# Down's first load as 116 rows and three times four rows, instead of 128 rows at once

## The chip, the cores and the metric

The kernel runs on one core of one Trainium2 chip. The metric is the device time of one execution in microseconds (us). A core has a matrix engine (PE), a vector engine (DVE), a scalar engine (ACT), GpSimd (POOL) and a queue engine (SP); loads from device memory are issued by SP or ACT and carried out by sixteen DMA engines that belong to the core.

## The reference

One token goes through a transformer block: a modulated layer norm, attention over a cache of 16384 keys and values for 32 heads, a second modulated layer norm, and a gated feed-forward part. Only the last line matters for the change.

```python
mod = (_silu(c) @ w_mod).reshape(c.shape[0], 6, 1, -1)
sa, ca, ga, sb, cb, gb = (mod[:, 0].copy(), ..., mod[:, 5].copy())
h = _layernorm(x, axis=-1) * (1 + ca) + sa
x = x + ga * _A_ref(h, A_k_cache, A_v_cache, A_wq, A_wo)      # attention; x is 1 x 1 x 640
h = _layernorm(x, axis=-1) * (1 + cb) + sb
g = _silu(h @ w_gate); u = h @ w_up                           # 640 x 1728 each
x = x + gb * (g * u @ w_down)                                 # w_down: 1728 x 640, "Down"
```

All matrices and the caches are bf16. The two caches are 134 MB each; the matrices together are about 22 MB.

## The kernel before, in words

The heads are worked in 16 pairs. A pair's keys (`kring`, two buffers) and values (`vbuf`) arrive as tiles of 128 partitions with 64 KB on each. DVE multiplies the keys by the query and folds the products, PE finishes the sums, ACT takes the exponentials, and PE weighs the values. PE's work on the pairs is a loop, and DVE's and ACT's from the third pair on.

All weights and caches are loaded by `dma` (line 83), which issues one load on SP's queue and gives it a semaphore of its own; the line that the profile names for every load is 90. SP issues in the order of the program and waits, ahead of a load, until its destination is free. The program has 44 such loads, all of 128 partition rows: w_mod, Wq, the first keys in two pieces, 15 more of keys, 16 of values, Wo in two pieces (line 631), Gate (642), Up (644) and five of Down (646 to 652). ACT issues the loads of `c` and `x`, one row each, and the second of the two stores of the result, which have two rows each (lines 770 and 771).

The tail is what the change touches. When the last keys have been reduced (`o_R[15]`), their buffer is free, and SP issues Gate, Up and the five loads of Down one behind the other (`wdeps`, line 641). Down's 1728 rows are cut by `BLOCKS` and `DOWN`. Each of the first three loads brings 512 rows of `w_down`, four to a partition: 128 partition rows of four times 640 values of two bytes, 5120 bytes each, 640 KB in all. The fourth has one row of `w_down` on each partition (160 KB), and the fifth has the last 64 rows, cut in half (80 KB).

Meanwhile PE weighs the last values, projects by Wo (line 679), and does Gate and Up (line 716). DVE makes `gu_col` from them (line 746). Then line 758 multiplies by Down in five parts, `down0` to `down4`; part i waits for load i. The first three parts have 16 matmuls each, the fourth and fifth have 4. `twice_gu` (763) and `gu_half` (765), which only `down4` needs, follow `down0`. DVE multiplies by the gate and adds the residual (767, 768), and SP and ACT each store half of the 640 results.

Of the kernel before, what the change touches and what calls it, by code (L numbers as in the profile page):

```python
# [37 lines left out]
class _Plan:  # L38
# [38 lines left out]
    def op(self, eng, fn, deps=(), name="", chan=None):  # L77
        o = _Op(eng, fn, list(deps), name, len(self.ops), self.loop.get(eng), chan)
        o.sig = chan is not None
        self.ops.append(o)  # L80
        return o

    def dma(self, out_ap, in_ap, key, deps=(), name="", eng="sp", noncontig=False):
        nc = self.nc

        def fn(e, out_ap=out_ap, in_ap=in_ap, noncontig=noncontig):
            if noncontig:
                with nc.allow_non_contiguous_dma(reason="tiny vector layout change"):
                    return e.dma_start(out_ap, in_ap)
            return e.dma_start(out_ap, in_ap)  # L90

        return self.op(eng, fn, deps, name, chan=self.dma_chan(key))
# [116 lines left out]
def build(nc, A_x, A_k, A_v, A_wq, A_wo, B_wg, B_wu, B_wd, c_in, w_mod, out):  # L209
# [13 lines left out]
    BLOCKS = [(0, 4, 0), (512, 4, 4), (1024, 4, 8), (1536, 1, 12)]  # L223

    DOWN = [(0, 0, 4), (1, 0, 4), (2, 0, 4), (3, 0, 1), (None, 0, 0)]
    FCH = NF + 1
    QW = 32
    QR = 16
# [4 lines left out]
    with es:  # L233
        plan = _Plan(nc, es)
        op, dma = plan.op, plan.dma
        POOL, ACT, DVE, PE = "pool", "act", "dve", "pe"

        def sb(name, shape, dtype):
            return es.enter_context(nc.sbuf_tensor(name, list(shape), dtype))
# [56 lines left out]
        ab = sb("ab", [128, KC, 2], BF16)  # L296
        g_sb = sb("g_sb", [128, FCH], F32)
        eg = sb("eg", [128, FCH], F32)
        dg = sb("dg", [128, FCH], F32)
        rg = sb("rg", [128, FCH], F32)  # L300
        sg = sb("sg", [128, FCH], F32)
        gu_col = sb("gu_col", [128, FCH], BF16)
        gu_half = sb("gu_half", [128, 2], BF16)
# [116 lines left out]
        def wide(col):  # L420
            return col.broadcast_to([col.shape[0], 32])
# [11 lines left out]
        def pick(half, n, o_m, free):  # L433
# [14 lines left out]
            deps=[o_m0, o_xn], name="t1")  # L448
# [11 lines left out]
        for g in range(H // 4):  # L460
            b = g % 2
# [9 lines left out]
            for half in range(2):  # L471
# [4 lines left out]
                    deps=[o_q[g]], name="qbc%d_%d" % (g, half)))  # L476
# [5 lines left out]
        o_R, o_pv, o_exp, o_nb, o_mx, o_acc, o_ot = ([None] * NP for _ in range(7))  # L482
# [141 lines left out]
        PL = NP - 1  # L624
# [16 lines left out]
        wdeps = [o_R[NP - 1]]  # L641
# [3 lines left out]
        d_wd = []  # L645
        for i, (b, r0, r1) in enumerate(DOWN):
            if b is None:
                dst, src = wt_v, B_wd[NF * 128:F, :].rearrange("q (h n) -> (q h) n", h=2)
            else:
                f0, n, j0 = BLOCKS[b]  # L650
                dst, src = wd_v[:, j0 + r0:j0 + r1, :], B_wd[f0:f0 + 128 * n, :].rearrange("(p r) n -> p r n", r=n)[:, r0:r1, :]
            d_wd.append(dma(dst, src, ("wd", i), deps=wdeps, name="dma_wd%d" % i))

# [2 lines left out]
                 deps=[o_exp[PL], o_rz, o_onesf, o_rstd], name="L")  # L658
# [7 lines left out]
                  deps=[o_z, o_e32] + o_qev[-2], name="am")  # L666
# [21 lines left out]
        def f_cols(e):  # L688
# [14 lines left out]
            deps=[o_ga, o_xf], name="x1")  # L703
# [18 lines left out]
        def gate0(o_xc1):  # L722
# [6 lines left out]
            deps=[o_xc1, o_rstd1, o_onep_b], name="t2")  # L729
# [6 lines left out]
                  deps=[o_xsp, o_ot[PL], o_strips], name="x1_rows")  # L736
# [9 lines left out]
        o_gum = op(DVE, lambda e: e.tensor_tensor(out=gu_col[:], in0=u_ps[:, 0:FCH], in1=sg[:], op=ALU.mult), deps=[o_sg, o_u], name="gu")  # L746
        for i, (b, r0, r1) in enumerate(DOWN):

            if b is None:
                work = [(gu_half[:, r // 2:r // 2 + 1], wt_v[:, RW * (r % 2):RW * (r % 2) + RW], r) for r in range(4)]  # L750
            else:
                j0 = BLOCKS[b][2]
                work = [(gu_col[:, j:j + 1], wd_v[:, j, RW * r:RW * r + RW], r) for j in range(j0 + r0, j0 + r1) for r in range(4)]

            def f_down(e, i=i, work=work):
                last = None
                for at, (col, rows, r) in enumerate(work):
                    last = e.matmul(f_ps[32 * r:32 * r + 32, 0:RW], lhsT=wide(col), rhs=rows, start=(i == 0 and at < 4),  # L758
                                    stop=(i == len(DOWN) - 1 and at >= len(work) - 4), tile_position=(0, 32 * r))
                return last  # L760
            prev = op(PE, f_down, deps=[o_gum if b is not None else o_guh, d_wd[i], o_nb[PL]], name="down%d" % i)
            if i == 0:
                o_tw = op(PE, lambda e: e.matmul(attn_ps[:, 8:9], lhsT=twice[64:128].rearrange("p q h -> p (q h)"), rhs=gu_col[64:128, NF:FCH], start=True, stop=True),
                          deps=[o_gum, o_twice, o_abf], name="twice_gu")
                o_guh = op(DVE, lambda e: e.tensor_tensor(out=gu_half[:], in0=attn_ps[:, 8:9].broadcast_to([128, 2]), in1=even[:], op=ALU.mult),
                           deps=[o_tw, o_even], name="gu_half")
# [10 lines left out]
def bass_adaLN_cond__gqa_block_cached__swiglu_ffn__decode_kernel(  # L777
    nc: bass.Bass,
    A_x: bass.AP,
    A_k_cache: bass.AP,  # L780
    A_v_cache: bass.AP,
    A_wq: bass.AP,
    A_wo: bass.AP,
    B_x: bass.AP,
    B_w_gate: bass.AP,
    B_w_up: bass.AP,
    B_w_down: bass.AP,
    c: bass.AP,
    w_mod: bass.AP,
    out: bass.AP,  # L790
):
    build(nc, A_x, A_k_cache, A_v_cache, A_wq, A_wo, B_w_gate, B_w_up, B_w_down, c, w_mod, out)
# [28 lines left out]
```

## Time and profile before

| | before |
|---|---|
| median of 3 runs | 679.24 us (678.79 to 679.37) |
| the profiled execution | 678.87 us |
| its span, first to last instruction | 677.6 us |
| DVE busy | 514.1 us (76%) |
| PE busy | 363.6 us (54%) |
| DMA: bytes, mean rate | 290.58 MB, 429 GB/s |
| DMA packets | 6355 |

The page of the profile gives busy time by engine, the span in 40 slices, the DMA queues with their packets, and the chain of work that ended last. Busy shares are of the span. A packet is one piece that one DMA engine moves; the end mark that tells a semaphore that the engine is done is a packet of 4 bytes. The DMA share of a window is the mean over the sixteen engines, so that 1.00 means that all are busy and 0.25 that four are, or that all are busy a quarter of the time. Windows and the timeline count from the span's start.

### The profile page before, as it was taken

What the parts mean: (1) busy time and instruction counts of PE and PEld (TensorE: products, weight loads), DVE (VectorE), ACT (ScalarE), POOL (GpSimd) and SP (SyncE); (2) the same over time, 40 slices, a digit from 0 to 9 for tenths busy, and PEclk for the clock granted to TensorE, in tenths of its full rate; (3) what the DMA queues carried; (4) which work ended last, traced back from release to release, by engine and by line L of the source; (5) the groups of instructions that cost most, each with busy time, mean ns of one, the idle gap of its engine ahead of it and who ended that gap; (6) DMA issues with size and microseconds to landing.
All of it is one profiled execution on the core that took longest, in us unless ns stands there. A gap on an engine that the chain in (4) does not pass through costs nothing.

```text
span 677.6 us, 5406 instructions
## 1 busy us (share of the span) xinstructions
PE 363.6 (54%) x2069; PEld 144.5 (21%) x2069; DVE 514.1 (76%) x190; ACT 46.4 (7%) x146; POOL 0.7 (0%) x6
## 2 busy tenths in 40 slices
PE   2420475755728284654818375562828465481776
PEld 1100122221212122221302122121212222130335
DVE  2189997959596896959597795959699695959912
ACT  1120000100000000000000010000000000000010
POOL 0000000000000000000000000000000000000000
PEclk9675565555757565565756556575656556565765
DMA  9999999999999999999999999999999999999997
GB/s 375 440 459 433 433 437 430 433 430 433 433 434 433 433 433 433 433 433 433 433 433 433 433 433 433 433 433 433 433 433 433 433 433 433 433 433 433 430 400 318
DMA packets 6355, 290.58 MB, mean 429 GB/s; under 512 B 714, under 2 KB 972, under 8 KB 1356
## 3 DMA queue, kind: packets, MB, share of 16 engines
q1 hardware_dynamic: 6340, 290.48, 99.3%
q8 instruction: 5, 0.08, 0.0%
q14 instruction: 2, 0.02, 0.0%
q10 hardware_dynamic: 8, 0.00, 0.0%
HBM read 290.47 MB, written 0.00 MB: 429 GB/s over the span
## 4 chain that ended last, share of the span: by engine, by line
DMA 49%; DVE 30%; issue 13%; PE 8%; SPq 0%; DVEq 0%
DMA kring<-in_A_k_cache_dram 45%; DVE kring L544 10%; PE psb L534 7%; DVE kring L549 6%; DVE kring L562 5%; DVE kring L568 5%; DMA kring<-in_B_w_down_dram 4%; DVE kring L554 3%; SPq L90 0%; DVE pm L581 0%; DVE nb L589 0%; PE psb L576 0%; PE psb L758 0%; DVEq L191 0%; DVEq L544 0%
## 5 line engine op out<-in xcount | busy, mean ns | idle before, releaser
L544 DVE TENSOR_TENSOR kring<-kring,qbc 128x16384 bf16<-128x16384 bf16 x28 | 243.3, 8690 | 96.1 <-DMA kring<-in_A_k_cache_dram 96.1
L534 PE MATMUL psb<-kring,ident 128*128 x448 | 197.5, 607 | 120.3 <-DVE kring L554 120.3
L549 DVE TENSOR_TENSOR kring<-kring 128x8192 bf16<-128x8192 bf16 x28 | 123.8, 4421 | 0.5
L534 PEld LDWEIGHTS psb<-kring,ident 128*128 128x128 bf16 x448 | 54.0, 120 | 248.0 <-issue 247.2
L508 PE MATMUL psb<-vbuf,PZ 128*8 128x512 bf16 x960 | 80.9, 511 | 0.0
L585 PE MATMUL psb<-d,bd_f 128*128 128x64 f32 x32 | 11.0, 446 | 118.5 <-ACT d L583 118.5
L554 DVE TENSOR_TENSOR kring<-kring 128x4096 bf16<-128x4096 bf16 x28 | 64.1, 2288 | 0.5
L562 DVE TENSOR_TENSOR kring<-kring,qbc 128x16384 bf16<-128x16384 bf16 (+2 forms) x5 | 34.9, 6981 | 23.4 <-DMA kring<-in_A_k_cache_dram 23.4
L508 PEld LDWEIGHTS psb<-vbuf,PZ 128*8 128x8 bf16 x960 | 26.6, 108 | 58.9 <-issue 49.0
L576 PE MATMUL psb<-kring,ident 128*128 128x256 bf16 (+3 forms) x64 | 14.5, 392 | 43.2 <-DVE kring L568 43.2
L585 PEld LDWEIGHTS psb<-d,bd_f 128*128 128x128 f32 x32 | 8.0, 312 | 120.7 <-DVE pm L581 111.3
L568 DVE TENSOR_TENSOR kring<-kring 128x2048 bf16<-128x2048 bf16 (+7 forms) x15 | 32.2, 2148 | 0.4
L523 PEld LDWEIGHTS psb<-sel,acc_sb 128*128 128x128 f32 x128 | 28.5, 311 | 7.7 <-issue 4.3
L523 PE MATMUL psb<-sel,acc_sb 128*128 128x2 f32 x128 | 25.6, 322 | 1.1 <-ACT acc_sb L514 1.1
L514 ACT ACTIVATE acc_sb<-psb 128x512 f32<-128x512 f32 x16 | 9.6, 598 | 210.7 <-PE psb L508 210.7
L593 ACT ACTIVATE PZ<-psb,nb 64x256 bf16<-64x256 f32 x32 | 15.0, 469 | 64.8 <-DVE nb L589 64.6
L576 PEld LDWEIGHTS psb<-kring,ident 128*128 128x128 bf16 x64 | 6.4, 121 | 50.5 <-DVE kring L568 44.3
L583 ACT ACTIVATE d<-negid,pm 128x64 f32<-128x64 f32 x16 | 5.6, 348 | 153.2 <-DVE pm L581 153.2
L466 PE MATMUL psb<-vbuf,h_col 128*128 128x512 bf16 x40 | 10.9, 443 | 8.6 <-DMA vbuf<-in_A_wq_dram 8.6
L527 ACT ACTIVATE OT_sb<-psb 128x2 f32 (+1 forms) x16 | 2.8, 172 | 152.2 <-PE psb L523 152.2
L581 DVE TENSOR_REDUCE pm<-psb 128x1 f32<-128x256 f32 x16 | 6.7, 419 | 1.2 <-PE psb L576 1.2
L466 PEld LDWEIGHTS psb<-vbuf,h_col 128*128 128x128 bf16 x40 | 4.1, 112 | 15.3 <-DMA vbuf<-in_A_wq_dram 9.0
(105 smaller groups left out, 79.2 us busy)
## 6 DMA issues: line engine op xcount, KB each, us to landing
kring<-in_A_k_cache_dram SPq DMA_DIRECT2D x2, 4096.0 KB, 40.1
vbuf<-in_A_wq_dram SPq DMA_DIRECT2D x1, 5120.0 KB, 25.8
kring<-in_w_mod_dram SPq DMA_DIRECT2D x1, 4800.0 KB, 14.1
vbuf<-in_A_wo_dram SPq DMA_DIRECT2D x1, 3200.0 KB, 20.6
kring<-in_B_w_gate_dram SPq DMA_DIRECT2D x1, 2160.0 KB, 20.6
kring<-in_B_w_up_dram SPq DMA_DIRECT2D x1, 2160.0 KB, 25.4
vbuf<-in_A_wo_dram SPq DMA_DIRECT2D x1, 1920.0 KB, 24.8
kring<-in_B_w_down_dram SPq DMA_DIRECT2D x3, 640.0 KB, 27.6
```

The source lines that it names most:

```text
L466: last = e.matmul(q_ps[b][:, 0:512], lhsT=h_col[:, k:k + 1].broadcast_to([128, 128]), rhs=wq_v[:, k, g * 512:(g + 1) * 512], start=(k == 0 ...
L508: last = e.matmul(acc_ps[32 * s:32 * s + 8, :], lhsT=PZ[:, j, :], rhs=v_at(p)[:, 4 * j:4 * j + 4, :].rearrange("p t d -> p (t d)"), start= ...
L523: last = e.matmul(OT_ps[:, 0:2], lhsT=acc_sb[:, 128 * i:128 * (i + 1)], rhs=sel[:, i:8:4], start=(i == 0), stop=(i == 3))
L534: last = e.matmul(S_ps[:, 0:T2], lhsT=ident[:], rhs=kring[:, bass.ds(plan.slot(p), 1), :, d].rearrange("p o t -> p (o t)"), start=(d == 0) ...
L544: return e.tensor_tensor(out=kv4, in0=kv4, in1=q4, op=ALU.mult)
L549: o_f = op(DVE, lambda e: e.tensor_tensor(out=kv4[:, :, 0], in0=kv4[:, :, 0], in1=kv4[:, :, 1], op=ALU.add), deps=[o_m], name="fold%d_%d" ...
L554: return op(DVE, lambda e: e.tensor_tensor(out=lo[:, :, 0:QR], in0=lo[:, :, 0:QR], in1=lo[:, :, QR:QW], op=ALU.add), deps=[o_f], name="fol ...
L562: o = op(DVE, lambda e: e.tensor_tensor(out=kv, in0=kv, in1=qbc[:, p, :].unsqueeze(1).broadcast_to([128, n, 128]), op=ALU.mult), deps=[d_k ...
L568: o = op(DVE, lambda e, w=w: e.tensor_tensor(out=kv[:, :, 0:w], in0=kv[:, :, 0:w], in1=kv[:, :, w:2 * w], op=ALU.add), deps=[o], name="fol ...
L576: last = e.matmul(S_ps[:, a:b], lhsT=ident[:], rhs=kring[:, p % 2, a:b, d], start=(d == 0), stop=(d == 15))
L585: o_mx[p] = op(PE, lambda e: e.matmul(mx_ps[:, 0:64], lhsT=bd_f[:], rhs=d2[:], start=True, stop=True), deps=[o_d2, o_bd1, o_bd2, o_nb[p - ...
L593: o_exp[p] = op(ACT, lambda e, half=half, ps=ps: e.activation(out=PZ[ps, :, 4 * half:4 * half + 4], in_=S_ps[ps, 0:T2].rearrange("p (c i) ...
```

## The change

The first of Down's five loads is cut in four along the partitions: rows 0 to 115, 116 to 119, 120 to 123 and 124 to 127. The four loads stand on SP's queue where the one stood, each with a semaphore of its own, and `down0` waits for all four. The other four loads of Down are issued as before, one each, behind them. The bytes, their places in the buffer and the arithmetic are the same. The change is described as "one load of 116 rows and three of four rows, which the lowest four DMA engines share".

```diff
+    UNEVEN = [0, 116, 120, 124, 128]
...
-            d_wd.append(dma(dst, src, ("wd", i), deps=wdeps, name="dma_wd%d" % i))
+            cuts = UNEVEN if i == 0 else [0, 128]
+            d_wd.append([dma(dst[a:b], src[a:b], ("wd", i, a), deps=wdeps, name="dma_wd%d_%d" % (i, a)) for a, b in zip(cuts, cuts[1:])])
...
-            prev = op(PE, f_down, deps=[o_gum if b is not None else o_guh, d_wd[i], o_nb[PL]], name="down%d" % i)
+            prev = op(PE, f_down, deps=[o_gum if b is not None else o_guh, o_nb[PL]] + d_wd[i], name="down%d" % i)
```

## The prediction

> **What bounds the kernel now.** I read the page first. Its slices show the DMA engines full from the first slice to the last, so the time is 290 MB at their rate plus whatever stands behind the last byte.
>
> ```profile
> span 677.6 us, 5406 instructions
> DMA  9999999999999999999999999999999999999997
> DMA packets 6355, 290.58 MB, mean 429 GB/s; under 512 B 714, under 2 KB 972, under 8 KB 1356
> q1 hardware_dynamic: 6340, 290.48, 99.3%
> q10 hardware_dynamic: 8, 0.00, 0.0%
> ```
>
> Next the chain of work that ended last, from 671 us on. The third load of Down, issued at 645.86, lands at 674.51. From there 1.08 us of matmuls and two DVE steps lead to the store.
>
> ```profile
> 645.86 28.65 DMA kring<-in_B_w_down_dram
> 674.51 0.04 issue
> 674.55 1.08 PE psb L758 x14
> 675.63 0.02 issue
> 675.65 0.34 DVE qbc L767
> 675.99 0.02 issue
> 676.01 0.24 DVE o_row L768
> ```
>
> The timeline of the tail shows what PE does around that landing. The first two parts of Down run as soon as `gu_col` is there; the third stands until its load has landed.
>
> ```profile
> 672.39 0.17 DVE L746 TENSOR_TENSOR gu_col<-psb,sg 128x14 bf16<-128x14 f32 x1 [2.77 <-PE psb L716]
> 672.61 0.73 PE L758 MATMUL psb<-kring,gu_col 128*32 128x160 bf16 x16 [0.34 <-DVE gu_col L746]
> 673.27 0.18 PE L763 MATMUL psb<-gu_col,twice 64*128 64x1 bf16 x1
> 673.38 0.72 PE L758 MATMUL psb<-kring,gu_col 128*32 128x160 bf16 x16
> 673.49 0.16 DVE L765 TENSOR_TENSOR gu_half<-psb,even 128x2 bf16<-128x2 f32 x1 [0.93 <-PE psb L763]
> 674.55 0.86 PE L758 MATMUL psb<-kring,gu_col 128*32 128x160 bf16 x20 [0.44 <-DMA kring<-in_B_w_down_dram]
> 675.28 0.33 PE L758 MATMUL psb<-kring,gu_half 128*32 128x160 bf16 x4
> 676.28 0.33 SPq L90 DMA_DIRECT2D out_dram<-o_row  x1
> ```
>
> Last, windows over the end of the loads: the stretch, the engines' busy times, the granted clock, and then the DMA share and GB/s.
>
> ```profile
> 670.00:672.00 2.00, 2.00 (x66) 2.00 (x65) 0.00 (x0) 0.00 (x0) 0.00 (x0) 0.50 1.01 412
> 672.80:673.50 0.70, 0.70 (x23) 0.44 (x19) 0.01 (x1) 0.00 (x0) 0.00 (x0) 0.50 0.90 319
> 673.50:674.00 0.50, 0.50 (x16) 0.28 (x12) 0.15 (x1) 0.00 (x0) 0.00 (x0) 0.50 0.37 138
> 674.00:674.40 0.40, 0.11 (x4) 0.00 (x0) 0.00 (x0) 0.00 (x0) 0.00 (x0) 0.50 0.29 101
> 674.40:674.80 0.40, 0.25 (x10) 0.25 (x14) 0.00 (x0) 0.00 (x0) 0.00 (x0) 0.50 0.16 48
> ```
>
> The engines do not end together. All sixteen are busy until about 673; then 0.37 x 16 = 5.9, 4.6 and 2.6 of them are. A load has landed only when its slowest engine has, so a few late engines set the end.
>
> **How many engines a load uses.** The packet counts tell it. SP's queue (q1) carried 44 loads of 128 rows and one store of two rows. With 128 packets of data and 16 end marks a load makes 144; 44 x 144 = 6336, and the store's two rows with two marks make 6340, the row above. ACT's queue (q10) had two loads of one row and a store of two: (1+1) + (1+1) + (2+2) = 8, the row above. So 128 rows went to sixteen engines with eight each, two rows to two, one row to one: each time the engines that took part had equal shares. 116 is 4 x 29 and is divisible by no other number from 3 to 16. With equal shares the large load runs on four engines with 29 rows each, and each load of four on four engines with one row. These are the same lowest four, going by the words of the change: 32 rows each, where every engine had 8. The other bound is unequal shares, 7 or 8 rows on every engine. I take equal shares, since all counts above are of that kind.
>
> [...]
>
> **The change part by part.**
>
> *The price of a row.* From 670 to 672 us only 5120-byte rows of Down move, at 412 GB/s with all engines busy. Sixteen rows take 16 x 5120 B / 412 GB/s = 0.199 us, so an engine moves one in 0.199 us. The old load takes 8 x 0.199 = 1.59 us of every engine. The new one takes 32 x 0.199 = 6.36 us of four engines and nothing of twelve. The four are 24 x 0.199 = 4.77 us behind where they were, the twelve 1.59 us ahead.
>
> *What hides it.* Nothing does. All later loads of Down need all sixteen engines, each engine works through its own in order, and the last landing is the end of the chain already. Gate and Up stand ahead of Down in the queue, so their landings and PE's work up to 672.6 stay.
>
> *PE.* `down0` now stands until the four engines have their 32 rows, some 3 to 4 us after 672.61. Behind it on PE wait `down1`, `twice_gu` and so `gu_half`. Between the landings of loads 0 and 2 lie two loads of 1.59 us, 3.2 us. Into these fit 0.73 + 0.18 + 0.72 us of PE work and the 0.16 us of `gu_half`, so the third load is still what ends last, and the 1.08 + 0.34 + 0.24 us and the store behind it are as before. Without that cover the PE parts would cost at most 1.6 us. Three more waits ahead of `down0` stand in a wait that is there anyway.
>
> *SP's queue.* Three more loads are issued.
>
> ```profile
> L90 SPq DMA_DIRECT2D kring<-in_B_w_down_dram x5: 432/432/1264, 644.9 to 646.8; - x5
> kring<-in_A_v_cache_dram SPq DMA_DIRECT2D x1, 38.9
> kring<-in_B_w_gate_dram SPq DMA_DIRECT2D x1, 2160.0 KB, 20.6
> 608.47 0.33 SPq L90 DMA_DIRECT2D kring<-in_A_v_cache_dram  x1
> 644.07 0.33 SPq L90 DMA_DIRECT2D kring<-in_B_w_gate_dram  x1
> ```
>
> (The five issues by their shortest, median and longest time in ns; two loads with their time to landing; their issues.) At 0.43 us and a little between, three more issues put Down's later loads off by 1.4 us. The engines come to them some 22 us after their issue, so that costs nothing. But the fifth issue took 1.26 us. It was the tenth load in flight, and ended at 648.1, shortly after the last values had landed (608.47 + 38.9 = 647.4). If the queue holds nine loads, the last one of Down, now thirteenth, has to wait until Gate has landed, at 644.07 + 20.6 = 664.7. The twelve engines that are ahead reach it at about 671, so 6 us of cover remain; and were it later still, the four slow engines reach it only after 678.
>
> *The sum.* If one of the late engines is among the four, the third load lands 4.77 us later and all behind it moves along: 678.87 + 4.77 = 683.64 for the profiled execution. The median of the runs stands 0.37 us above that execution, so 679.24 + 4.77 = **684.0 us**.
>
> **Which engines are late** is the unknown. Shares times lengths after 672.8 sum to 0.90 x 0.7 + 0.37 x 0.5 + 0.29 x 0.4 + 0.16 x 0.4 = 0.995 us, times 16 engines 15.9 us. One of these engines was reading program code:
>
> ```profile
> q8 instruction: 1, 0.02, 2.4%
> ```
>
> This is the window 673.2 to 676.0, so 0.024 x 16 x 2.8 = 1.08 us of one engine. That leaves 14.8 us. With four late engines until 674.7, 7.6 us in all, the other twelve have 7.2 / 12 = 0.6 us each: they end at 673.4 on average, 1.3 us ahead of the late ones. No view names the engine of a packet.
>
> **The rivals.**
>
> *A* (the forecast): at least one late engine is among the lowest four, +4.77 us, 684.0. If lateness falls on engines by chance, four of sixteen miss the late four with (12 x 11 x 10 x 9) / (16 x 15 x 14 x 13) = 27%, so this holds in 73%.
>
> *B*: none is. Then the four start from an earlier line, the worst of them about 1.0 us (0.6 to 1.6) ahead of the late ones: 4.77 - 1.0 = +3.8 us, 683.0 (682.4 to 683.4). The late ones, relieved by 1.59 us, do not matter. [...]
>
> *C*: a code load falls on one of the four while they still work. One takes 1.08 us of an engine by the row above, and one comes at about 673, in reach of the longer tail. 684.0 + 1.1 = 685.1, up to 685.4.
>
> *D* (the change does not do what it says): 116 rows go to all engines with 7 or 8 each, and only the three small loads to the lowest four, 11 rows for 8. At most 3 x 0.199 = +0.6 us, 679.8; about 679.1 if the four are early, since the others lose a row or none. Against it: every count of marks above comes from equal shares.
>
> *E* (faster): an engine's rate is a sixteenth of a shared limit, and four engines alone run faster. From 671.6 to 674.5 they would have 2.9 us for some 7.7 us of rows at today's rate, so it decides from 2.6 times that rate on; at three times the end comes 0.3 us before today's, 678.9, and only at some five times would it be faster by over 0.2%. Against it: when 4.6 engines were busy they moved 101 GB/s, 22 GB/s each with smaller rows, and at 5.9 engines 138 GB/s, 23 each; with all sixteen it is 412 / 16 = 26 each. Fewer engines did not mean faster ones.
>
> **How the numbers follow.** Equal shares hold with about 0.92. Of this A has 0.56, B 0.25, C 0.09 and a stall of the queue that I have not seen 0.02. D has 0.06 and E 0.02. A, B, C and the stall are slower by over 0.2% (1.4 us, about what a measurement of this kernel can tell from no change): 0.92. D is within, and so is E up to five times the rate: 0.06 + 0.01. The rest of E is faster: 0.01. The range takes in B's lower end and C's upper end with the runs' own spread of 0.2 us: 682.2 to 685.4; D and E lie outside.
>
> **What the next profile would show.** q1 again has 6340 packets (43 x 144 + 116 + 4 + 3 x 8 + 4); 6352 would be rival D. The DMA share falls from 1.0 to about 0.25 at some 672 to 673 us and stays there for about 5 us. The first two matmul groups of line 758 stand behind a DMA until after 675. The chain still ends in a load of Down, then 1.08 us of line 758. Gate and Up are at the same times as now. I am wrong if the share of 0.25 has a clearly higher rate per engine than 26 GB/s, if it does not appear, or if the last of Down's loads is issued late enough to land behind the slow engines.

## The result and the profile after

The changed kernel takes 685.69 us (median of six runs, 685.45 to 686.22), the kernel before 679.16 us, also of six runs: 1.0098 times as long, 95% interval 1.0085 to 1.0111. That is 6.5 us more, where 4.8 were forecast, and 0.3 us above the upper end of the range. The way was right and the size was not.

The profiled execution took 686.02 us with a span of 684.8. Its page has the same packets as before, which is what equal shares on four engines leave (rival D would have left 6352 on q1):

```profile
span 684.8 us, 5410 instructions
DMA packets 6355, 290.58 MB, mean 424 GB/s; under 512 B 714, under 2 KB 972, under 8 KB 1356
q1 hardware_dynamic: 6340, 290.48, 98.6%
```

The chain of work still ends in the third load of Down. It lands at 681.70 and not at 674.51, and what follows is as before:

```profile
648.73 32.97 DMA kring<-in_B_w_down_dram
681.70 0.04 issue
681.74 1.07 PE psb L760 x18
682.82 0.02 issue
682.84 0.34 DVE qbc L769
683.17 0.02 issue
683.20 0.24 DVE o_row L770
```

The timeline shows PE in front of the loads. Up (L718) waits longer than before and starts at 670.70, not 669.85; the first part of Down (L760) waits until 678.73:

```profile
670.70 2.44 PE L718 MATMUL psb<-h_col,kring 128*128 128x1 bf16 x70 [2.34 <-DMA kring<-in_B_w_up_dram]
678.73 0.73 PE L760 MATMUL psb<-kring,gu_col 128*32 128x160 bf16 x16 [5.60 <-DMA kring<-in_B_w_down_dram]
679.61 0.16 DVE L767 TENSOR_TENSOR gu_half<-psb,even 128x2 bf16<-128x2 f32 x1 [6.20 <-PE psb L765]
680.18 0.73 PE L760 MATMUL psb<-kring,gu_col 128*32 128x160 bf16 x16 [0.61 <-DMA kring<-in_B_w_down_dram]
681.74 0.86 PE L760 MATMUL psb<-kring,gu_col 128*32 128x160 bf16 x20 [0.83 <-DMA kring<-in_B_w_down_dram]
```

The windows over the loads (last columns: granted clock, DMA share, GB/s) hold the surprise:

```profile
669.00:674.00 5.00, 2.44 (x70) 2.35 (x70) 0.72 (x4) 0.12 (x1) 0.00 (x0) 0.50 0.98 222
674.00:676.00 2.00, 0.00 (x0) 0.00 (x0) 0.00 (x0) 0.00 (x0) 0.00 (x0) 0.50 0.49 133
676.00:680.00 4.00, 0.84 (x17) 0.54 (x17) 0.16 (x1) 0.00 (x0) 0.00 (x0) 0.50 0.26 105
```

From 676 to 680 us four engines are busy (0.26 x 16 = 4.2) and move 105 GB/s, 25 GB/s each. That is the forecast tail of four engines at their old rate. But from 669 to 674 all sixteen are busy and move 222 GB/s together, where the same engines moved 412 before: a row of Down takes 5120 B x 16 / 222 GB/s = 0.37 us on average and not 0.20. In these 5 us an engine that gets its sixteenth moves 13.6 rows in place of 25.1. The 11.6 rows that are missing make 11.6 x 0.199 = 2.3 us, if the four engines that set the end are as slow as the average of all sixteen. That is an estimate, and it leaves out what follows: from 674 to 676 the 0.49 x 16 = 7.8 busy engines move 17 GB/s each, which by the same reckoning adds up to 0.7 us.

### The profile page after: what moved, and what is told of

It reads as the page before. It is cut to its first block, busy times and chain, and to the rows that moved or that the text cites. A ratio compares the mean times of both kernels' runs of the same rounds, so it can differ in the third digit from the quotient of the medians.

```text
span 684.8 us, 5410 instructions
## 1 busy us (share of the span) xinstructions
PE 360.1 (53%) x2069; PEld 143.3 (21%) x2069; DVE 514.1 (75%) x190; ACT 46.4 (7%) x146; POOL 0.7 (0%) x6
## 4 chain that ended last, share of the span: by engine, by line
DMA 49%; DVE 30%; issue 13%; PE 8%; SPq 1%; DVEq 0%
DMA kring<-in_A_k_cache_dram 44%; DVE kring L545 10%; PE psb L535 7%; DVE kring L550 6%; DVE kring L563 5%; DMA kring<-in_B_w_down_dram 5%; DVE kring L569 5%; DVE kring L555 3%; SPq L90 1%; DVE pm L582 0%; DVE nb L590 0%; PE psb L577 0%; PE psb L760 0%; DVEq L191 0%; DVEq L545 0%
## 5 line engine op out<-in xcount | busy, mean ns | idle before, releaser
L509 PE MATMUL psb<-vbuf,PZ 128*8 128x512 bf16 x960 | 79.5, 504 | 0.0
## 6 DMA issues: line engine op xcount, KB each, us to landing
vbuf<-in_A_wo_dram SPq DMA_DIRECT2D x1, 3200.0 KB, 19.7
kring<-in_B_w_gate_dram SPq DMA_DIRECT2D x1, 2160.0 KB, 20.6
```

Of the source, the lines that this page charges most:

```text
L509: last = e.matmul(acc_ps[32 * s:32 * s + 8, :], lhsT=PZ[:, j, :], rhs=v_at(p)[:, 4 * j:4 * j + 4, :].rearrange("p t d -> p (t d)"), start= ...
```

## The experiments

Why does every engine slow down while the four are at work beside the others? Three theories stood at the start. *Memory*: the four engines read 29 rows one behind the other, 148 KB apart from each other, and their reads collide with those of the others in device memory. *Ports*, which rests on an assumption that no view shows: a load of 128 rows gives each engine a place of its own among the partitions, and a load of 116 rows sends four engines over places where others are writing. *Constant price*: rows are not slowed by the split, and late engines and a code load explain the time. Each comparison below is with the kernel before on the same chip; the diffs are against the changed kernel.

**The same cut at 112.** Sixteen engines can share 112 rows.

```diff
-    UNEVEN = [0, 116, 120, 124, 128]
+    UNEVEN = [0, 112, 116, 120, 124, 128]
```

> The large load has 112 rows, which sixteen engines can share evenly with 7 each, and four loads of four rows follow; the lowest four engines have 11 rows, the others 7. Three theories of why a row took up to 0.4 us in place of 0.2 us after the change. Memory (the four engines' reads, 148 KB apart, collide with the others' reads): no slow rows here, the four have three rows more and the others one less; since the four are not the late ones, 679.0 to 679.3 us, within 0.2% of before. Ports (engines write to partitions that other engines are writing next to): blocks of 7 rows no longer fall on each engine's own partitions, so rows slow down in this load as well, up to 1.6 us, 679.5 to 680.8. Constant price (the rows are not slower because of the split, a code load and late engines explain the rest): 679.0 to 679.8.

It took 681.83 us against 679.36, ratio 1.0039 (1.0025 to 1.0054): +2.5 us. From 669 to 674 all engines were busy at about the rate of the change:

```profile
669.00:674.00 5.00, 2.43 (x70) 2.35 (x70) 0.68 (x4) 0.19 (x1) 0.00 (x0) 0.50 0.97 231
```

So rows are slow too where all sixteen engines are at work (share 0.97) and 112 rows make seven for each of them. Memory and constant price do not give that. Ports give the direction, but the time lies above the 1.6 us that I had allowed. The four small loads, one row on each of the lowest four engines, may add to the loss; this run does not part them from the large load.

**Halves.** Each of Down's first three loads is cut into its lower and its upper 64 rows.

```diff
-            cuts = UNEVEN if i == 0 else [0, 128]
+            cuts = [0, 64, 128] if i <= 2 else [0, 128]
```

> Down's first three loads are each cut into the lower 64 and the upper 64 rows; every load runs on all sixteen engines with four rows each, so all engines have the same work as before. [...] Memory: the reads are the same 640 KB in two contiguous halves, no change, 679.0 to 679.5. Constant price: no change, 679.0 to 679.5.

683.83 us, ratio 1.0074 (1.0058 to 1.0091): +4.5 us, though every engine has exactly the rows that it had before (q1 has 6388 packets, 48 more, the sixteen end marks of three more loads). The rate is 229 GB/s with all engines busy, for 8 us:

```profile
669.00:677.00 8.00, 3.82 (x101) 3.19 (x98) 1.33 (x7) 0.41 (x2) 0.00 (x0) 0.50 1.00 229
```

Memory and constant price expected no change. Of the three theories only Ports, in which it matters where an engine writes, leaves room for this loss.

**Another source.** The load of 116 rows reads from Wq, at other addresses and distances.

```diff
-            d_wd.append([dma(dst[a:b], src[a:b], ...
+            other = A_wq[0:116, 0:4 * D].rearrange("p (r n) -> p r n", r=4)
+            d_wd.append([dma(dst[a:b], other if b == 116 else src[a:b], ...
```

> The change as it is, but the load of 116 rows reads its rows from Wq (rows 8192 bytes apart) and not from Down; the rest of the work is the same, and 464 of Down's 1728 rows are left out of the result. Memory: other addresses and other distances, so the collision goes or becomes another one: between 683.0 and 684.0 if it goes. Ports: the same writes, 685.5 to 686.0. Constant price: 685.5 to 686.0.

686.13 us, ratio 1.0102 (1.0085 to 1.0119), the change's own time, and 231 GB/s in its window:

```profile
669.00:674.00 5.00, 2.42 (x70) 2.34 (x70) 0.77 (x4) 0.31 (x2) 0.00 (x0) 0.50 1.00 231
```

Where the rows came from did not matter here.

**The cut in the third load.** The four engines keep their 32 rows, but have little company.

```diff
-            cuts = UNEVEN if i == 0 else [0, 128]
+            cuts = UNEVEN if i == 2 else [0, 128]
```

> The cut of 116, 4, 4 and 4 is made in the third of Down's loads and not in the first. The twelve other engines have then only 160 and 80 KB to share behind it, some 0.7 us, so the four engines do most of their 32 rows alone. If slow rows need other engines at work beside the four (memory or ports): 0.199 us a row for most of them, 683.0 to 684.0. Constant price with a code load on one of the four: as after, 685.5 to 686.0, since the four have the same rows in all.

683.56 us, ratio 1.0062 (1.0045 to 1.0079): +4.2 us, inside what was expected where slow rows need company. The windows show the full rate until 671 us, and then four engines at 0.26 x 16 = 4.2 engines' worth and 108 GB/s, 26 GB/s each, which is the old 0.2 us a row:

```profile
670.00:671.00 1.00, 1.00 (x31) 1.00 (x32) 0.00 (x0) 0.00 (x0) 0.00 (x0) 0.50 1.01 410
674.00:677.00 3.00, 0.56 (x16) 0.23 (x8) 0.00 (x0) 0.00 (x0) 0.00 (x0) 0.50 0.26 108
677.00:678.00 1.00, 0.00 (x0) 0.00 (x0) 0.00 (x0) 0.00 (x0) 0.00 (x0) 0.50 0.25 97
678.00:679.00 1.00, 0.00 (x0) 0.00 (x0) 0.00 (x0) 0.00 (x0) 0.00 (x0) 0.50 0.13 47
```

Constant price falls here: the four have the same rows and the time is 2.1 us less. A price on the mere number of loads falls with it, since the same eight loads of Down are issued.

**The middle 64 rows and the lower 64.** Two kernels with loads of the same sizes, which differ in where the 64 rows lie.

```diff
-            cuts = UNEVEN if i == 0 else [0, 128]
+            cuts = [0, 32, 96, 128] if i <= 1 else [0, 128]     # e5_middle
+            cuts = [0, 64, 96, 128] if i <= 1 else [0, 128]     # e6_lower
```

> Down's first two loads are cut into rows 0 to 31, 32 to 95 and 96 to 127; every piece runs on all sixteen engines, with 2, 4 and 2 rows each, so each engine has its 8 rows. [...] Cost of more and smaller loads, wherever they lie: the same as the next kernel, e6_lower.

> The same two loads cut into rows 0 to 63, 64 to 95 and 96 to 127: the same sizes and the same number of loads as e5_middle, only the 64 rows lie elsewhere. [...] Cost of more and smaller loads: the same as e5_middle within 0.4 us.

682.17 us, ratio 1.0047 (1.0030 to 1.0064), and 683.79 us, ratio 1.0070 (1.0053 to 1.0087). The difference, 1.6 us, is more than the 0.4 us that the number and the size of the loads allowed, but the two intervals overlap. From 669 to 674 the rates are 254 and 213 GB/s:

```profile
669.00:674.00 5.00, 2.40 (x70) 2.33 (x70) 0.59 (x3) 0.37 (x2) 0.00 (x0) 0.50 0.99 254
```

```profile
669.00:674.00 5.00, 1.88 (x58) 1.88 (x59) 0.59 (x3) 0.24 (x2) 0.00 (x0) 0.50 0.97 213
```

Both are far below the 404 to 412 of the kernel before. Which of its three pieces are slow, no view of e5_middle tells. Engines end up to two microseconds apart in the kernel before (share 0.90 from 672.8 to 673.5 us, 0.16 from 674.4 to 674.8), so while some write the middle piece others may be in the pieces of 32 rows. The pair did not decide, so the next runs add one load to the kernel before and leave its own loads whole.

**One engine that visits.** 29 rows on a single engine, ahead of Down's loads.

```diff
+        xd = kb[:, wd0 + NF * D + D // 2:wd0 + NF * D + D // 2 + 4 * D].rearrange("p (r n) -> p r n", r=4)
+        d_xd = dma(xd[0:29], B_wd[0:512, :].rearrange("(p r) n -> p r n", r=4)[0:29], "extra", deps=wdeps, ...)
...
-            cuts = UNEVEN if i == 0 else [0, 128]
+            cuts = [0, 128]
```

> The kernel before with one more load of 29 rows of Down, which nothing uses, ahead of Down's first: 29 has no divisor up to 16, so it goes to one engine, which writes over the other engines' places one after the other, as each of the four does in the change. If only the engine whose place is visited loses: the rate with all engines busy falls by at most a sixteenth or two, to 360 to 400 GB/s, and the time is 684 to 686 (29 rows of 0.199 us and some at half rate, on an engine that may be up to 1 us ahead of the late ones). If writes at a visited place hold up all engines, as the 230 GB/s of the change suggest: below 330 GB/s at full DMA share.

685.13 us, ratio 1.0084 (1.0067 to 1.0101): +5.9 us, within the time expected for a local loss. On q1 stand 6370 packets, 30 more than before: 29 rows and one end mark, so one engine. Then the same with 128 rows, aligned on all engines (`xd[0:128]`):

> The kernel before with one more load of 128 rows of Down, which nothing uses, ahead of Down's first: eight rows more for every engine, each on its own place. All theories: 8 x 0.199 = +1.6 us, 680.9, and the rate stays at 400 GB/s or more. It shows what an additional load costs where neither shares nor places are uneven.

680.77 us, ratio 1.0022 (1.0013 to 1.0032): +1.5 us, so another load costs its bytes. The rates in the same stretch, with all engines busy, of the single visitor, of the aligned load and of the kernel before:

```profile
669.00:673.00 4.00, 2.44 (x70) 2.35 (x70) 0.94 (x6) 0.41 (x2) 0.00 (x0) 0.50 1.00 366
```

```profile
669.00:673.00 4.00, 2.43 (x70) 2.35 (x70) 0.76 (x4) 0.39 (x2) 0.00 (x0) 0.50 1.01 419
```

```profile
669.00:673.00 4.00, 2.81 (x86) 2.73 (x86) 0.72 (x4) 0.12 (x1) 0.00 (x0) 0.50 1.00 404
```

One visitor takes 404 - 366 = 38 to 419 - 366 = 53 GB/s from the sum, one and a half to two engines' worth at 26 GB/s each. Four would take 152 to 212 and leave 252 to 207 GB/s; the change showed 222. So the change's low rate is about four times the loss that one visitor makes. That the four losses simply add up is an assumption.

**One load, two places.** The decisive pair: the same 64 rows of 12800 bytes from the same source, on sixteen engines with four rows each, once to partitions 32 to 95 and once to partitions 0 to 63. As in the two kernels above, nothing uses them. Both kernels have 6420 packets on q1, 80 more than before: 64 rows and sixteen end marks.

```diff
+        xd = kb[:, wd0 + NF * D + D // 2:wd0 + NF * D + D // 2 + 10 * D].rearrange("p (r n) -> p r n", r=10)
+        d_xd = dma(xd[32:96], B_wd[0:640, :].rearrange("(p r) n -> p r n", r=10), "extra", deps=wdeps, ...)    # e9
+        d_xd = dma(xd[0:64], B_wd[0:640, :].rearrange("(p r) n -> p r n", r=10), "extra", deps=wdeps, ...)     # e10
...
-            cuts = UNEVEN if i == 0 else [0, 128]
+            cuts = [0, 128]
```

> The kernel before with one more load ahead of Down's first, of 64 rows of 12800 bytes (819 KB), which nothing uses, written to partitions 32 to 95; sixteen engines take four rows each. [...] If 64 rows are slow wherever they lie: as e10_extra_lower.

> The same load with the same source, written to partitions 0 to 63. [...] If 64 rows are slow wherever they lie, or fast wherever they lie: as e9_extra_middle within 0.4 us.

681.00 us, ratio 1.0027 (1.0016 to 1.0038): +1.7 us, a little less than the 2.0 us of its bytes (819 KB at 412 GB/s). And 685.76 us, ratio 1.0102 (1.0084 to 1.0121): +6.4 us, 4.8 us more than the middle rows, where 0.4 was allowed if the place made no difference. The windows of the middle load:

```profile
669.00:672.00 3.00, 1.95 (x60) 1.95 (x61) 0.59 (x3) 0.36 (x2) 0.00 (x0) 0.50 0.97 403
672.00:675.00 3.00, 1.31 (x32) 0.92 (x30) 0.33 (x2) 0.00 (x0) 0.00 (x0) 0.50 1.01 399
```

and of the lower one, with the same bytes and the same engines:

```profile
669.00:672.00 3.00, 0.00 (x0) 0.00 (x0) 0.59 (x3) 0.15 (x1) 0.00 (x0) 0.50 0.91 142
672.00:675.00 3.00, 2.36 (x70) 2.35 (x70) 0.00 (x0) 0.00 (x0) 0.00 (x0) 0.50 0.98 215
675.00:678.00 3.00, 0.33 (x14) 0.28 (x14) 0.17 (x1) 0.00 (x0) 0.00 (x0) 0.50 1.00 357
668.00:676.00 8.00, 2.83 (x79) 2.53 (x76) 1.17 (x6) 0.41 (x2) 0.00 (x0) 0.50 1.00 195
```

The view counts a packet, with all its bytes and its time, in the window in which it begins, so short windows are rough where packets are long; the last row is the whole slow stretch.

Only the destination's partitions differ: 403 GB/s in the one case, 142 to 215 and 195 over the whole stretch in the other. For these 64 rows that shows the destination to be the cause, by itself. For the 116 rows of the change the cause rests on several runs together: another source made no difference, little company took the slow rows away, and a single visitor made a loss of the right size. No run moved the 116 rows to other partitions. Why partitions 32 to 95 kept the rate and 0 to 63 did not, no run shows.

## Why the prediction was wrong in size

*How many engines a load uses*: right. Packets and a tail of 4.2 busy engines show four engines for the 116 rows. Rival D fell with it.

*The price of a row*: this step failed. The 0.199 us came from a window in which only loads of 128 rows ran, and I carried it to loads of 116 and four rows beside them. I put the slowing at nothing, though nothing in the profile of before showed a load with other shares. The price held where the four engines were alone (25 to 26 GB/s each) and was 0.37 us on average beside the others. So the share of 0.25, forecast from 672 to 673 on, came only at 676. The run with the cut in the third load measures the term of the sum without this: +4.2 us for the uneven shares with little company, which lies between the forecasts with a late engine among the four (+4.77) and without (+3.8). The change took 6.5 us, so the slow rows cost 6.5 - 4.2 = 2.3 us. The estimate from the rate, 2.3 us and up to 0.7 more, has the same size; that its first part agrees to the tenth is luck.

*What hides it*: right that nothing does, wrong that Up would stay. Up landed later, presumably because its last rows ran beside the first of the four engines' rows, and PE began it 0.85 us later. That cost nothing, since the first part of Down waited until 678.7 anyway.

*PE*: right. `down1`, `twice_gu` and `gu_half` ran between the landings, and the chain behind the third load has the same 1.07, 0.34 and 0.24 us.

*SP's queue*: right that it costs nothing, wrong in the reason. SP stood in its issues much longer, up to 4.5 us in one (the first row gives shortest, median and longest in ns):

```profile
L90 SPq DMA_DIRECT2D kring<-in_B_w_down_dram x8: 290/1310/4521, 644.9 to 657.5; - x8
644.92 17.01 SPq L90 DMA_DIRECT2D kring<-in_B_w_down_dram  x8
```

The last issue ended at 644.92 + 17.01 = 661.9, well before an engine came to it. But a queue that holds nine loads is not the reason. In the run of the halves SP also issued eight loads of Down behind Gate and Up, and no issue took over 0.60 us, though Gate, issued at 644.47, landed only 20.6 us later and so all ten were in flight; with the one visitor, six loads were enough for an issue of 12.6 us:

```profile
L90 SPq DMA_DIRECT2D kring<-in_B_w_down_dram x8: 432/594/597, 645.3 to 649.7; - x8
L90 SPq DMA_DIRECT2D kring<-in_B_w_down_dram x6: 333/432/12640, 645.2 to 652.3; - x6
```

What does set the length of an issue stays open.

*Which engines are late*: not settled. In the run with the cut in the third load the share falls from 0.25 to 0.13 at about 678 us, so two of the four end about a microsecond before the other two; no view says whether these two are late ones of before.

*Rivals C and E*: C stays open. One code load did begin between 669 and 674 us, with 1.7% of sixteen engines' 5 us, 1.4 us of one engine; no view tells whether that was one of the four, and no run tried it alone:

```profile
q8 instruction: 1, 0.02, 1.7%
```

The rows were slow on all sixteen engines at once (share 0.98, and no row of 5120 bytes that began from 669 to 674 took under 0.27 us), which a load on one engine does not explain; but it may have added to the end. E, a higher rate for few engines, fell: four engines moved 105 and 108 GB/s, one in e7_one 26:

```profile
676.00:680.00 4.00, 1.51 (x33) 0.94 (x33) 0.16 (x1) 0.00 (x0) 0.00 (x0) 0.50 0.06 26
```

## What to carry to other kernels

Before a load is cut along its partitions, ask how many engines share the new row count evenly, and to which partitions the pieces go beside the loads that run at the same time. The price per row that was read where only loads of 128 rows ran did not hold here beside other pieces: with 116 rows on four engines it nearly doubled (0.199 to 0.37 us), and halves of 64 rows, with perfectly even shares, cost 4.5 us over three loads. If a load must have 64 rows: as one more load beside loads of 128 rows, partitions 32 to 95 kept the full rate here (403 GB/s) and 0 to 63 did not (195); beside pieces of 32 rows, 32 to 95 did not keep it either (254 GB/s).

## What the runs showed of the hardware

- A DMA share of 1.0 does not mean the full rate. At shares of 0.97 to 1.00 the engines moved 195 to 254 GB/s in the runs that cut a load or wrote 64 lower rows, and 399 to 419 with a load of 128 rows or of the middle 64 added. At the low rate a packet takes longer: one of 5120 bytes took 0.35 us on average (0.28 to 0.53) from 669 to 674 us in the changed kernel, and 0.20 us (0.196 to 0.205) in the kernel before.
- One visiting engine took 38 to 53 GB/s from the sum, one and a half to two engines' worth (26 GB/s each). In two runs with loads of 64 rows the rate was near half of 412, which is 206: 229 GB/s in the halves and 195 with the lower 64 rows.
- The lower 64 rows, 819 KB, cost 6.4 us, though by themselves at half rate (206 GB/s) they would have cost 4.0. The rate stayed low for 8 us, and 8 x 195 GB/s is 1.56 MB: about half of what moved slowly were rows of Up and Down beside them. 8 x (1 - 195 / 412) = 4.2 us lost, and 2.0 us for the bytes, make 6.2.
- How long SP stands in its issues does not go by the number of loads. Eight loads of Down took 17.0 us in the change and 4.8 in the halves; six took 19.7 us with the 29 rows on one engine, 8.7 with the aligned 128 rows and 3.0 with the lower 64. In the change this fell between 645 and 662 us, when the DMA rate was not yet disturbed (417 GB/s in this stretch, 418 in the kernel before).
